# Attention with routed experts: one pair's transposes in each pair, VectorE's order written per pair

## The chip, the core and the metric

The kernel runs on one core of a Trainium2 chip. A core has engines with an instruction queue each: TensorE (PE; its weight loads are shown as PEld), VectorE (DVE), ScalarE (ACT), GpSimd (POOL) and SyncE (SP, which here only issues DMAs). They meet through semaphores. TensorE writes to PSUM, which has eight banks here handed out as named tiles. The metric is the device time of one execution in microseconds (us); lower is better.

## The reference

```python
scores = q @ k.T / sqrt(64); scores = cap * tanh(scores / cap)     # (8, 12, 448, 448)
attn = exp(scores - max) / (sum + 1e-9);  x = attn @ v             # x as (3584, 768)
logits = x @ w_gate + modality_bias[modality_id]                   # (3584, 8)
e_idx = argmax(logits); gate_w = softmax(logits)[e_idx]
for e in range(8):                                                 # 768 -> 1024 -> 768
    out[mask] = gate_w[mask, None] * (relu(x[mask] @ w1[e]) @ w2[e])
```

## The kernel before

**Attention** goes over 48 pairs of heads (g = 0 to 47; six pairs make a batch). Three pairs make a group h (HB = 3), two groups a batch; the odd group completes a batch, which is then routed. In pair g the four steps of the loop do this:

- Steps 0 and 2 issue the score matmuls of pair g (L453): queries and keys are split in a rounded part (hi) and the rest (lo), and three products are added. ScalarE takes each score block through tanh (L455, th) and exp (L457, pt, and sh for the keys that two heads share).
- Step 1 prepares pair g + 1 (prep: VectorE casts hi, L441, and subtracts lo, L442), adds up the exponentials of pair g - 1 (two additions to tot, L552 and L553), and multiplies them by the values (L462, weigh_own, into the PSUM tile xT).
- Step 3 adds the shared keys (L467, weigh_shared) and VectorE copies xT to SBUF (L572). The next pair's L462 needs that PSUM tile back. Then pair g + 2 is fetched.

A group of three pairs leaves over the next three pairs. In the first (r = 0) and second (r = 1), sums (L477) forms denominators and logits on TensorE (glog); at the end of the second, VectorE copies glog (L483), TensorE transposes it (L486, lt), and VectorE forms reciprocals and logits (L491, L494). For an odd group, route follows: a string of small VectorE operations (L210 to L234), and in the next pair a rank on TensorE (L238, L240), positions (L244 to L251), and four indirect writes to a map in DRAM by POOL (L264). In the third pair (r = 2), after L467, all three pairs are transposed (rows_out, L505, four transposes for each pair) and VectorE scales each result by the reciprocal into xs (L506); POOL then writes xs to DRAM (L515). The first and third set use the one PSUM buffer tp, the middle one the buffer "small", which rank and lt use too.

**The early slot.** After group 13 (pair 45), early_slot picks an expert that has a full block of rows. SP loads its first weights (raw; four buffers), POOL reads the map back (L653, mt) and gathers the rows (L660, xg). While the last pairs run, the weights are cast and split (split_w, L676 on ScalarE, L677 on VectorE; SPLITS says at which pair and step), and the gathered rows are transposed (L696; MOVES says where) into x (L703, L705, L706). Then the **experts** run (ffn1 L723 to L727, ffn2 L752), first with the early slot, then with the slots planned from the counts.

**What sets the order.** Python's order is the program's; the tile framework then orders each engine's instructions anew by its own estimates, except those marked with pin, which keep their order among each other. Before, all matmuls and DMAs issued by SP are pinned, and on VectorE only prep of the first two pairs and the early slot's casts. Tiles with n buffers (bufs) make the writer of the n + 1st wait for the readers of the first.

Of the kernel before, what the change touches and what calls it, by code (L numbers as in the profile page):

```python
# [39 lines left out]
F32 = mybir.dt.float32  # L40
# [4 lines left out]
ALU = mybir.AluOpType  # L45
# [4 lines left out]
B, H, S, D = 8, 12, 448, 64  # L50
C, CP = 4, 112
NP = H // 2
NT, DM, FF, E, NM = B * S, H * D, 1024, 8, 2
# [5 lines left out]
GW = 32  # L59
# [12 lines left out]
HB = 3  # L72
# [3 lines left out]
class Program:  # L76
# [7 lines left out]
    def pin(self, inst):  # L84
        return self.tc.keep_in_program_order(inst)
# [327 lines left out]
    def attention(self, qk, first, rp):  # L413
        tc, nc = self.tc, self.nc
        pe, pin = nc.tensor, self.pin
        with ExitStack() as st:
# [17 lines left out]
            def prep(g):  # L434
                kq, va = fetched.pop(g)
                hi = sp.tile([128, QK], F32R, name="hi")
                lo = sp.tile([128, QK], F32R, name="lo")
                keep = pin if g < 2 else (lambda inst: inst)

                for cs in (slice(0, QK),) if g else (slice(0, KC2), slice(KC2, QK)):  # L440
                    keep((nc.scalar.copy if cs.start else nc.vector.tensor_copy)(hi[:, cs], kq[:, cs]))  # L441
                    keep(nc.vector.tensor_tensor(lo[:, cs], kq[:, cs], hi[:, cs], op=ALU.subtract))  # L442
                return hi, lo, va
# [34 lines left out]

            def by_token():

                w = HB * GW
                gl = xp.tile([w, S], F32, name="gl")
                nc.vector.tensor_copy(gl, self.glog[:w, :S])  # L483
                lt = self.ps_r.tile([128, 512], F32, name="lt", tag="small")
                for c in range(C):
                    pin(pe.transpose(lt[:CP, c * w : (c + 1) * w], gl[:, c * CP : (c + 1) * CP], self.ident[:w, :w]))  # L486
                return lt[:CP, : C * w].rearrange("p (c t x) -> p c t x", c=C, t=HB)
# [11 lines left out]

            def rows_out(h, t, xs, rec):  # L500
                xT = kept.pop(h * HB + t)[0]
                pool, tag = (self.ps_r, "small") if t == 1 else (ps_v, "tp")
                tp = pool.tile([128, 512], F32, name="tp", tag=tag)
                for c in range(C):
                    pin(pe.transpose(tp[:CP, c * 128 : (c + 1) * 128], xT[:, c * CP : (c + 1) * CP], self.ident))  # L505
                nc.vector.tensor_tensor(  # L506
                    xs[:, :, t * 128 : (t + 1) * 128].rearrange("p c (j d) -> p c j d", j=2),
                    tp[:CP].rearrange("p (c j d) -> p c j d", c=C, j=2),
                    rec[:, :, t].unsqueeze(3).to_broadcast([CP, C, 2, D]),
                    op=ALU.mult,  # L510
                )

            def store(h, xs):
# [7 lines left out]
            SPLITS = {  # L521
                (NG - 2, 1): (0,),
                (NG - 2, 3): (1,),
                (NG - 1, 1): (2,),
                (NG - 1, 3): (3,),
                (NG - 0, 0): (4,),
                (NG - 0, 1): (5,),
            }
            MOVES = {(NG - 1, 3): (0, 1), (NG, 1): (2, 3), (NG, 3): (4, 5)}
            self.warm(self.ps_r, 4)  # L530
# [4 lines left out]
            fetch(1)  # L535
            kept, lgs, routing, raws = {}, {}, {}, []
            for g in range(NG + 1):
# [4 lines left out]
                for step in range(C):  # L542
# [3 lines left out]
                    if step == 1:  # L546
                        if g + 1 < NG:
                            ready = prep(g + 1)
                        if g:
                            ppt, psh, pva = pend  # L550
                            tot = xp.tile([128, 2, S], F32, name="tot", bufs=HB + 1)
                            nc.vector.tensor_tensor(tot, ppt[:, 0:2], ppt[:, 2:4], op=ALU.add)  # L552
                            nc.vector.tensor_tensor(tot, tot, ppt[:, 4:6], op=ALU.add)  # L553
                            xT = ps_x.tile([128, 512], F32, name="xT")
                            weigh_own(xT, ppt, pva)

                        if g > HB:
                            h, r = divmod(g - HB - 1, HB)
                            if r < 2:
                                sums(h, 2 * r)  # L560
                                sums(h, 2 * r + 1)
                    if step == 3:
                        if g in routing:
                            next(routing.pop(g), None)
                        if g == 3:
                            self.empty_map()
                        if g == 2:
                            self.gate_bias()
                        if g:
                            weigh_shared(xT, psh, pva)  # L570
                            xs_ = xp.tile([128, S], F32, name="xT", bufs=HB + 3)
                            nc.vector.tensor_copy(xs_, xT[:, :S])  # L572
                            kept[g - 1] = xs_, tot, psh
                        fetch(g + 2)
                        if g > HB:
                            h, r = divmod(g - HB - 1, HB)
                            b = h // NH
                            if r == 1:
                                if h % NH == 0:
                                    lgs[b] = xp.tile([CP, C, H, E], F32, name="lg")  # L580
                                lt = by_token()
                                rec = logits(h, lt, lgs[b])
                                if h % NH == NH - 1:
                                    way = self.route(b, lgs[b], rp, self.ps_r)
                                    next(way)
                                    routing[g + 1] = way
                            if r == 2:
                                xs = xp.tile([CP, C, HB * 128], F32, name="xs")
                                for t in range(HB):
                                    rows_out(h, t, xs, rec)  # L590
                                store(h, xs)
                                if h == NH * (B - 1) - 1:
                                    meta = self.early_slot(self.cpool, self.ps_r)
                    for k in SPLITS.get((g, step), ()):
# [7 lines left out]
                if g == NG - 3:  # L602
                    e = self.expert(meta, 0)
                    early = e, self.rows(meta, 0)
                    raws = [self.load_raw(e, self.w1, k, FF) for k in range(self.nstage)]
                if g == NG - 2:
                    self.gather(early[1], known=NT - S)
            self.raws = [self.load_raw(e, self.w2, k, DM) for k in range(self.nstage)]
            h = NG // HB - 1
            for part in range(4):  # L610
                sums(h, part)
            rec = logits(h, by_token(), lgs[B - 1])
            way = self.route(B - 1, lgs[B - 1], rp, self.ps_r)
# [322 lines left out]
    def build(self):  # L936
        tc, nc = self.tc, self.nc
        with ExitStack() as st:
# [4 lines left out]
            with ExitStack() as sa:  # L943
                qk = sa.enter_context(tc.tile_pool(name="qk", bufs=3))
                first = self.load_kq(qk, 0, parts=2)
# [90 lines left out]
```

## Time and profile before

| | us |
|---|---|
| runs | 1011.59, 1011.34, 1003.75 (median 1011.34) |
| the profiled execution | 1000.3 |
| its span, first to last instruction | 998.6 |
| PE busy in the span | 923.6 (92%) |
| DVE busy | 542.2 (54%) |
| ACT busy | 555.5 (56%) |
| POOL busy | 132.6 (13%) |
| mean granted clock of TensorE | 0.972 |

The span has two stages: attention up to about 469, the experts from there on. A row of a list gives line, engine, operation, what is written and read, count, busy time and mean duration, and after the bar the idle time of the engine ahead of these instructions and what ended it. A row of the timeline starts with start and duration; in brackets stands the idle time before it and its releaser. A busy TensorE is not TensorE at its peak, since the ends of matmuls are modelled.

### The profile page before, as it was taken

Reading aid. Unit: us, or ns where it says so; the run is one execution under the profiler, and the core shown is the slowest. Engines: PE = TensorE matmul, PEld = TensorE weight load, DVE = VectorE, ACT = ScalarE, POOL = GpSimd, SP = SyncE. Lnnn points to the kernel's source line nnn. Section 1 sums busy time; section 2 is a strip of 40 time slices with the busy share of each in tenths; the row PEclk is TensorE's granted clock in tenths of the full one; section 3 lists DMA queues with packets and bytes.
Section 4 is the critical chain, followed back from the end, with each engine's and each line's share of the span. In section 5 each row is a group of like instructions: output and inputs, shape, how many; then the busy total and the mean of one; then the engine's idle time right before and its main releaser. Section 6 shows DMA issues by size and latency. Waiting matters only on the chain. (4 is left out here: it accounts for less than half of the span.)

```text
span 998.6 us, 14505 instructions
## 1 busy us (share of the span) xinstructions
PE 923.6 (92%) x5360; PEld 709.6 (71%) x5360; DVE 542.2 (54%) x940; ACT 555.5 (56%) x759; POOL 132.6 (13%) x145
## 2 busy tenths in 40 slices
PE   8898989999898989876989999999999999999997
PEld 3444444444444444434879999999999999998987
DVE  5657676656556676646644444343434343428762
ACT  6877778867676777762334443443434443436551
POOL 1001002020202011031242020202020202011100
PEclk9999999999899999988999999999999999999998
DMA  3422424233233423264376363536353545347660
GB/s 114 133 90 92 140 99 118 96 113 119 89 119 85 123 91 121 97 155 138 92 254 226 123 209 118 206 132 199 131 193 131 182 145 182 131 137 248 230 199 6
DMA packets 47176, 139.98 MB, mean 140 GB/s; under 512 B 8686, under 2 KB 9198, under 8 KB 47088
## 3 DMA queue, kind: packets, MB, share of 16 engines
q1 hardware_dynamic: 38000, 105.78, 32.2%
q0 software_dynamic: 8944, 33.10, 11.0%
q8 instruction: 46, 0.75, 0.3%
q14 instruction: 42, 0.34, 0.1%
q10 hardware_dynamic: 144, 0.00, 0.0%
HBM read 117.35 MB, written 22.69 MB: 140 GB/s over the span
## 5 line engine op out<-in xcount | busy, mean ns | idle before, releaser
L455 ACT ACTIVATE th<-sc,isc 128x896 f32<-128x896 f32 x192 | 167.1, 907 | 105.8 <-PE sc L453 105.8
L727 PE MATMUL ph<-x,al 128*128 128x384 f32 (+2 forms) x528 | 167.9, 318 | 0.0
L752 PE MATMUL py<-bh,hh 128*128 128x384 f32 x464 | 159.6, 344 | 2.9 <-ACT hh L733 2.3
L752 PE MATMUL py<-bh,hl 128*128 128x384 f32 x464 | 156.0, 337 | 0.0
L752 PE MATMUL py<-bl,hh 128*128 128x384 f32 x464 | 155.7, 336 | 0.0
L457 ACT ACTIVATE pt<-th,cabs 128x896 f32<-128x896 f32 x144 | 148.0, 1043 | 1.9
L462 PE MATMUL xT<-pt,va 128*64 128x448 f32 x576 | 126.1, 575 | 6.5 <-DVE xT L572 6.5
L723 PE MATMUL ph<-x,ah 128*128 128x384 f32 x384 | 129.5, 337 | 0.5 <-DVE hl L734 0.5
L724 PE MATMUL ph<-x,ah 128*128 128x384 f32 x384 | 129.2, 336 | 0.0
L552 DVE TENSOR_TENSOR tot<-pt 128x896 f32<-128x896 f32 x48 | 52.4, 1091 | 122.3 <-ACT pt L457 68.9
L677 DVE TENSOR_TENSOR bl<-raw,bh 128x768 fp32r<-128x768 f32 x88 | 81.4, 955 | 56.2 <-ACT bh L676 55.4
L676 ACT CAST bh<-raw 128x768 fp32r<-128x768 f32 x88 | 70.2, 839 | 63.9 <-DMA raw<-in_w_dram 55.7
L727 PEld LDWEIGHTS ph<-x,al 128*128 128x128 f32 x528 | 102.1, 193 | 0.0
L453 PE MATMUL sc<-hi 64*128 64x448 f32 (+1 forms) x336 | 90.7, 469 | 6.7 <-ACT th L455 6.1
L677 DVE TENSOR_TENSOR al<-raw,ah 128x1024 fp32r<-128x1024 f32 x66 | 78.8, 1222 | 28.7 <-ACT ah L676 28.2
L453 PEld LDWEIGHTS sc<-hi 64*128 64x128 f32 (+1 forms) x336 | 38.4, 198 | 75.8 <-ACT pt L457 27.4
L462 PEld LDWEIGHTS xT<-pt,va 128*64 128x64 f32 x576 | 39.1, 144 | 74.6 <-issue 55.0
L752 PEld LDWEIGHTS py<-bh,hh 128*128 128x128 f32 x464 | 87.5, 189 | 4.0 <-ACT hh L733 2.9
L757 ACT ACTIVATE ot<-py,mt 128x384 f32<-128x384 f32 x58 | 33.6, 580 | 100.4 <-PE py L752 51.4
L752 PEld LDWEIGHTS py<-bl,hh 128*128 128x128 f32 x464 | 87.7, 189 | 0.0
L752 PEld LDWEIGHTS py<-bh,hl 128*128 128x128 f32 x464 | 87.5, 189 | 0.1
L676 ACT CAST ah<-raw 128x1024 fp32r<-128x1024 f32 x66 | 66.6, 1048 | 33.4 <-DMA raw<-in_w_dram 31.8
(159 smaller groups left out, 1302.8 us busy)
## 6 DMA issues: line engine op xcount, KB each, us to landing
raw<-in_w_dram SPq DMA_DIRECT2D x66, 512.0 KB, 5.1
raw<-in_w_dram SPq DMA_DIRECT2D x88, 384.0 KB, 4.8
kq<-in_kq_dram SPq DMA_DIRECT2D x47, 480.0 KB
va<-in_v_dram SPq DMA_DIRECT2D x48, 256.0 KB, 2.7
xd<-xs POOLq DMA_DIRECT2D x16, 672.0 KB
mapd<-pay,pos POOLq DMA_INDIRECT x32
xg<-xd,mt POOLq DMA_INDIRECT x30
out_dram<-ot,mt POOLq DMA_INDIRECT x29
```

The source lines that it names most:

```text
L453: pin(pe.matmul(sc[:, j, :S], k[rows, ks], q[rows, KC2:], start=i == 0, stop=i == 2))
L455: nc.scalar.activation(th[:, :n], sc[:, :n, :S], AF.Tanh, scale=self.isc)
L457: nc.scalar.activation(dst, th[:, :n] if step < KU else th[:, 0], AF.Exp, scale=self.cabs)
L462: pin(pe.matmul(xT[j * D : (j + 1) * D, :S], va[:, u * D : (u + 1) * D], pt[:, u], start=u < 2, stop=False))
L552: nc.vector.tensor_tensor(tot, ppt[:, 0:2], ppt[:, 2:4], op=ALU.add)
L676: a = self.nc.scalar.copy(hi, raw)
L677: b = self.nc.vector.tensor_tensor(lo, raw, hi, op=ALU.subtract)
L723: nc.tensor.matmul(ph[:, :w], hi[:, fs], self.x[:, k, 0, :w], start=first, stop=False)
L724: nc.tensor.matmul(ph[:, :w], hi[:, fs], self.x[:, k, 1, :w], start=False, stop=False)
L727: nc.tensor.matmul(ph[:, :w], lo[:, fs], self.x[:, k, 0, :w], start=False, stop=last)
L752: nc.tensor.matmul(py[:, :HALF], self.h[a][:, f, rows], self.w2s[f][c][:, cs], start=i == 0, stop=i == 3 * FC - 1,)
L757: nc.scalar.mul(ot[:, cs], py[:, :HALF], mt[:, t, 1:2])
```

## The change

- rows_out transposes one pair in each pair of the loop, where it did three in every third: set t of group h in pair 3h + 6 + t, ahead of the shared product, always through tp. The three at once stay for groups 13, 14 and 15 (`burst`). The store follows the third.
- VectorE's casts, additions, evictions and copies in the pair loop are all pinned, so their order is that of the text: hi, lo, two additions, (copy of glog), eviction, xT.
- tot has five buffers instead of four, the kept xT seven instead of six, qk (the loads of queries and keys) two instead of three.
- The early slot's casts come one step or pair later, its transposes all in the last turn of the loop, and the gather is written right after the loads.

```diff
-                keep = pin if g < 2 else (lambda inst: inst)
...
-                    keep((nc.scalar.copy if cs.start else nc.vector.tensor_copy)(hi[:, cs], kq[:, cs]))
-                    keep(nc.vector.tensor_tensor(lo[:, cs], kq[:, cs], hi[:, cs], op=ALU.subtract))
+                    pin((nc.scalar.copy if cs.start else nc.vector.tensor_copy)(hi[:, cs], kq[:, cs]))
+                    pin(nc.vector.tensor_tensor(lo[:, cs], kq[:, cs], hi[:, cs], op=ALU.subtract))
...
+            def copy_sums():
+                gl = xp.tile([HB * GW, S], F32, name="gl")
+                pin(nc.vector.tensor_copy(gl, self.glog[: HB * GW, :S]))
+                return gl
...
-            def rows_out(h, t, xs, rec):
+            def rows_out(h, t, xs, rec, burst=True):
                 xT = kept.pop(h * HB + t)[0]
-                pool, tag = (self.ps_r, "small") if t == 1 else (ps_v, "tp")
+                pool, tag = (self.ps_r, "small") if burst and t == 1 else (ps_v, "tp")
...
             SPLITS = {
-                (NG - 2, 1): (0,),
-                (NG - 2, 3): (1,),
-                (NG - 1, 1): (2,),
-                (NG - 1, 3): (3,),
-                (NG - 0, 0): (4,),
-                (NG - 0, 1): (5,),
+                (NG - 2, 3): (0,),
+                (NG - 1, 1): (1,),
+                (NG - 1, 3): (2,),
+                (NG, 0): (3,),
+                (NG, 1): (4,),
+                (NG, 2): (5,),
             }
-            MOVES = {(NG - 1, 3): (0, 1), (NG, 1): (2, 3), (NG, 3): (4, 5)}
+            MOVES = {(NG, 1): (0, 1), (NG, 2): (2, 3), (NG, 3): (4, 5)}
...
+            LAST = NH * (B - 1) - 1
...
-                            tot = xp.tile([128, 2, S], F32, name="tot", bufs=HB + 1)
-                            nc.vector.tensor_tensor(tot, ppt[:, 0:2], ppt[:, 2:4], op=ALU.add)
-                            nc.vector.tensor_tensor(tot, tot, ppt[:, 4:6], op=ALU.add)
+                            tot = xp.tile([128, 2, S], F32, name="tot", bufs=HB + 2)
+                            pin(nc.vector.tensor_tensor(tot, ppt[:, 0:2], ppt[:, 2:4], op=ALU.add))
+                            pin(nc.vector.tensor_tensor(tot, tot, ppt[:, 4:6], op=ALU.add))
...
+                        h, t = divmod(g - 2 * HB, HB)
+                        if h >= 0 and (t == 0 or h < LAST):
+                            if t == 0:
+                                rec, xs = recs.pop(h), xp.tile([CP, C, HB * 128], F32, name="xs")
+                            for u in (t,) if h < LAST else range(HB):
+                                rows_out(h, u, xs, rec, h >= LAST)
+                            if t == HB - 1 or h >= LAST:
+                                store(h, xs)
+                            if h == LAST:
+                                meta = self.early_slot(self.cpool, self.ps_r)
                         if g:
                             weigh_shared(xT, psh, pva)
-                            xs_ = xp.tile([128, S], F32, name="xT", bufs=HB + 3)
-                            nc.vector.tensor_copy(xs_, xT[:, :S])
+                            xs_ = xp.tile([128, S], F32, name="xT", bufs=2 * HB + 1)
+                            pin(nc.vector.tensor_copy(xs_, xT[:, :S]))
...
-                if g == NG - 2:
                     self.gather(early[1], known=NT - S)
...
-                qk = sa.enter_context(tc.tile_pool(name="qk", bufs=3))
+                qk = sa.enter_context(tc.tile_pool(name="qk", bufs=2))
```

TensorE in the third pair of an odd group, before: sc are scores, tp the transposes of the kept xT, rank the routing's.

```order
L453 MATMUL sc<-lo,hi 128x448
L238 LDWEIGHTS tri
L238 MATMUL rank<-oh,tri 112x32
L240 LDWEIGHTS ones
L240 MATMUL rank<-before,ones 112x32
L467 MATMUL xT<-sh,va 128x448
L505 MATMUL tp<-ident,xT 112x128 x12
L453 MATMUL sc<-hi 128x448 x2
```

The same place in the changed program:

```order
L452 MATMUL sc<-lo,hi 128x448
L238 LDWEIGHTS tri
L238 MATMUL rank<-oh,tri 112x32
L240 LDWEIGHTS ones
L240 MATMUL rank<-before,ones 112x32
L507 MATMUL tp<-ident,xT 112x128 x4
L466 MATMUL xT<-sh,va 128x448
L452 MATMUL sc<-hi 128x448 x2
```

Eight of the twelve transposes have left for the next two pairs, and the four that stay stand ahead of the shared product.

VectorE in that pair, before: acc ends the routing's string, rows and posf are its positions, xs the evictions.

```order
L552 TENSOR_TENSOR tot<-pt 128x896
L234 TENSOR_TENSOR acc<-before,oh 112x8
L259 TENSOR_REDUCE gs<-ex 112x4
L260 TENSOR_SCALAR gs<-gs 112x4
L441 CAST hi<-kq 128x960
L244 TENSOR_TENSOR rows<-rank,region 112x32
L261 RECIPROCAL pay<-gs 112x4
L442 TENSOR_TENSOR lo<-kq,hi 128x960
L247 TENSOR_TENSOR rows<-rows,oh 112x32
L572 COPY xT<-xT 128x448
L249 TENSOR_REDUCE posf<-rows 112x4
L506 TENSOR_TENSOR xs<-tp,rec 112x4x128
```

And in the changed program:

```order
L234 TENSOR_TENSOR acc<-before,oh 112x8
L440 CAST hi<-kq 128x960
L260 TENSOR_SCALAR gs<-gs 112x4
L441 TENSOR_TENSOR lo<-kq,hi 128x960
L555 TENSOR_TENSOR tot<-pt 128x896
L261 RECIPROCAL pay<-gs 112x4
L556 TENSOR_TENSOR tot<-tot,pt 128x896
L244 TENSOR_TENSOR rows<-rank,region 112x32
L508 TENSOR_TENSOR xs<-tp,rec 112x4x128
L247 TENSOR_TENSOR rows<-rows,oh 112x32
L588 COPY xT<-xT 128x448
```

Both additions now stand between lo and xT, and one eviction ahead of xT; the routing's string still stands ahead of hi.

ScalarE in pair 46, before: ah is the first cast of the early slot's weights.

```order
L457 ACTIVATE pt<-th,cabs 128x896
L676 CAST ah_149<-raw 128x1024
L455 ACTIVATE th<-sc,isc 128x896
L455 ACTIVATE th<-sc,isc 128x448
L457 ACTIVATE pt<-th,cabs 128x896
L457 ACTIVATE sh<-th,cabs 128x448
L676 CAST ah_151<-raw 128x1024
```

And in the changed program, from the end of pair 46 into pair 47:

```order
L456 ACTIVATE pt<-th,cabs 128x896
L456 ACTIVATE sh<-th,cabs 128x448
L682 CAST ah_149<-raw 128x1024
L454 ACTIVATE th<-sc,isc 128x896 x2
L456 ACTIVATE pt<-th,cabs 128x896 x2
L682 CAST ah_151<-raw 128x1024
```

The first cast has moved behind all of pair 46's activations.

More of the change, by code (lines that the diff above doesn't have):

```diff
@@ L477, in sums, with by_token @@
                     pin(pe.matmul(self.glog[t * GW : (t + 1) * GW, :S], w, rhs, start=part == 0, stop=part == 3))
-            def by_token():
+            def copy_sums():
+                gl = xp.tile([HB * GW, S], F32, name="gl")
+                pin(nc.vector.tensor_copy(gl, self.glog[: HB * GW, :S]))
+                return gl
+            def by_token(gl):
                 w = HB * GW
-                gl = xp.tile([w, S], F32, name="gl")
-                nc.vector.tensor_copy(gl, self.glog[:w, :S])
                 lt = self.ps_r.tile([128, 512], F32, name="lt", tag="small")
@@ L505, in rows_out @@
                     pin(pe.transpose(tp[:CP, c * 128 : (c + 1) * 128], xT[:, c * CP : (c + 1) * CP], self.ident))
-                nc.vector.tensor_tensor(
+                pin(nc.vector.tensor_tensor(
                     xs[:, :, t * 128 : (t + 1) * 128].rearrange("p c (j d) -> p c j d", j=2),
@@ L510, in rows_out @@
                     op=ALU.mult,
-                )
+                ))
             def store(h, xs):
@@ L535, in attention @@
             fetch(1)
-            kept, lgs, routing, raws = {}, {}, {}, []
+            kept, lgs, recs, routing, raws = {}, {}, {}, {}, []
+            LAST = NH * (B - 1) - 1
             for g in range(NG + 1):
@@ L561, in attention @@
                                 sums(h, 2 * r + 1)
+                                if r:
+                                    gl = copy_sums()
                     if step == 3:
@@ L569, in attention @@
                         if g:
                             weigh_shared(xT, psh, pva)
-                            xs_ = xp.tile([128, S], F32, name="xT", bufs=HB + 3)
-                            nc.vector.tensor_copy(xs_, xT[:, :S])
+                            xs_ = xp.tile([128, S], F32, name="xT", bufs=2 * HB + 1)
+                            pin(nc.vector.tensor_copy(xs_, xT[:, :S]))
                             kept[g - 1] = xs_, tot, psh
                         fetch(g + 2)
-                        if g > HB:
-                            h, r = divmod(g - HB - 1, HB)
+                        h, r = divmod(g - HB - 1, HB)
@@ L577, in attention @@
+                        if h >= 0 and r == 1:
                             b = h // NH
[L578 to L593, printed above, removed]
+                            if h % NH == 0:
+                                lgs[b] = xp.tile([CP, C, H, E], F32, name="lg")
@@ L594, in attention @@
+                            recs[h] = logits(h, by_token(gl), lgs[b])
+                            if h % NH == NH - 1:
+                                way = self.route(b, lgs[b], rp, self.ps_r)
+                                next(way)
+                                routing[g + 1] = way
                     for k in SPLITS.get((g, step), ()):
@@ L611, in attention @@
                 sums(h, part)
-            rec = logits(h, by_token(), lgs[B - 1])
+            rec = logits(h, by_token(copy_sums()), lgs[B - 1])
             way = self.route(B - 1, lgs[B - 1], rp, self.ps_r)
```

## The prediction

> **What bounds the kernel now.** I read the busy time by stage first: from the first transposes of sums (L486, at 54.64) to those of group 13 (413.60), and on to the first matmul of the experts (469.16). The columns are the stretch, its length, then busy time and instructions of PE, PEld, DVE, ACT and POOL, the granted clock, the DMA share and GB/s.
>
> ```profile
> 54.64:413.60 358.96, 324.29 (x1899) 164.65 (x1897) 228.15 (x401) 266.70 (x319) 39.76 (x43) 0.96 0.34 108
> 413.60:469.16 55.56, 39.59 (x221) 19.43 (x219) 33.93 (x71) 29.78 (x38) 12.34 (x11) 0.88 0.51 144
> ```
>
> TensorE (PE) is busy 90% of the attention stage, VectorE (DVE) 64%, ScalarE (ACT) 74%: TensorE sets the pace, and what stops it counts. The experts' 529 us behind 469.16 are not touched, so the change can win only in these two rows. Next, who stops TensorE between 54.64 and 413.60, from the list of waits:
>
> ```profile
> PE tp L505 <- DVE xs L506: 25.9, 13, 2.2
> PE xT L462 <- DVE xT L572: 4.0, 13, 0.3
> PE tp L505 <- DVE rows L244: 3.5, 6, 0.6
> PE rank L240 <- DVE before L233: 1.2, 6, 0.2
> ```
>
> That is 34.6 us, the whole of TensorE's idle time there (358.96 - 324.29 = 34.67). 29.4 of it stands before the three pairs' transposes (tp). The timeline shows why, in a pair in which an even group leaves:
>
> ```profile
> 219.99 0.47 PE L453 MATMUL sc<-hi 64*128 64x448 f32 x2
> ...
> 226.13 1.04 PE L505 MATMUL tp<-ident,xT 128*112 128x128 f32 x8
> 226.28 0.65 DVE L441 CAST hi<-kq 128x960 fp32r<-128x960 f32 x1
> 226.97 1.16 DVE L442 TENSOR_TENSOR lo<-kq,hi 128x960 fp32r<-128x960 f32 x1
> 228.04 0.62 DVE L572 COPY xT<-xT 128x448 f32<-128x448 f32 x1
> 228.57 1.28 DVE L506 TENSOR_TENSOR xs<-tp,rec 112x512 f32<-112x512 f32 x2
> 229.31 0.65 PE L505 MATMUL tp<-ident,xT 128*112 128x128 f32 x4 [2.15 <-DVE xs L506]
> 229.89 0.47 PE L453 MATMUL sc<-hi 64*128 64x448 f32 x2
> ...
> 231.31 0.97 PE L462 MATMUL xT<-pt,va 128*64 128x448 f32 x4
> ```
>
> The third set of transposes needs the first set's buffer, whose reader (xs, at 228.57) stands behind hi, lo and xT on VectorE. Then the groups one by one, from L486 to L486:
>
> ```profile
> 54.64:82.41 27.77, 25.31 (x147) 12.93 (x146) 16.06 (x23) 20.46 (x25) 0.90 (x1) 0.94 0.31 107
> 82.41:109.66 27.25, 24.32 (x149) 12.21 (x148) 19.30 (x42) 20.60 (x26) 6.03 (x6) 1.00 0.35 109
> ...
> 164.63:190.88 26.25, 23.81 (x147) 12.05 (x145) 16.06 (x23) 20.46 (x25) 0.72 (x1) 1.00 0.35 113
> 190.88:219.57 28.69, 25.79 (x149) 13.31 (x148) 19.30 (x42) 20.59 (x26) 5.64 (x6) 0.94 0.36 104
> ...
> 245.83:275.97 30.14, 27.24 (x148) 13.62 (x147) 19.27 (x42) 20.57 (x26) 5.30 (x6) 0.89 0.30 99
> ...
> 385.85:413.60 27.75, 25.29 (x147) 12.90 (x145) 16.05 (x23) 20.46 (x25) 0.72 (x1) 0.94 0.31 107
> ```
>
> There are 13 such rows, two kinds in turn: seven even ones, and six odd ones, whose batch is routed (42 VectorE instructions instead of 23). At a granted clock of 1.00 (six rows) an even one takes 26.25 and an odd one 27.25; at 0.94 (six rows) each is some 1.45 longer, at 0.89 (one row) 2.9. So eight slowdowns cost about 8 x 1.45 = 11.8 us (358.96 - 7 x 26.25 - 6 x 27.25 = 11.7).
>
> **The change part by part.**
>
> *Transposes in each pair.* No instruction is added or removed: 12 transposes and three evictions a group before and after. What goes is the wait for the buffer: 2.15 in an even group (the row at 229.31); in an odd one 25.9 - 7 x 2.15 = 10.9, or 1.8, and 3.5 / 6 = 0.6 for the rank that shares a buffer with the middle set. Since the buffer now has a whole pair to come free, I put the new wait at nothing. The cover is the pair itself: its shortest form is 219.99 to 226.13 on TensorE (6.1 us), and the eviction takes 0.64.
>
> *VectorE's order per pair.* It is now hi, lo, both additions, eviction, xT. The rows above give hi 0.65, lo 1.16, xT 0.62 and an eviction 0.64 (1.28 for two); the additions' groups:
>
> ```profile
> L552 DVE TENSOR_TENSOR tot<-pt 128x896 f32<-128x896 f32 x39 | 42.6, 1091 | 110.7 <-ACT pt L457 60.6 <-PE glog L477 50.1
> L553 DVE TENSOR_TENSOR tot<-tot,pt 128x896 f32<-128x896 f32 x39 | 41.5, 1063 | 0.0
> ```
>
> Together 5.2 us a pair, under the 6.1 of the shortest pair. xT, for which the next pair's L462 waits, was 0.3 late once a group; now the only work behind the shared product (L467) is xT itself, 0.62 against the 1.4 us of the next score matmuls (229.89 to 231.31 in the rows above). So that 4.0 goes too. The fifth tot buffer removes the 50.1 that VectorE waited for glog (L477), and that TensorE never felt: worth nothing alone, but without it the fixed order would hold xT behind an addition that waits for the group before.
>
> *The price of the order: routing.* In an odd group the routing's small operations now run ahead of hi in one queue. Their length, from the trace of before:
>
> ```profile
> 415.35 0.30 DVE L491 RECIPROCAL rec<-lt 112x24 f32<-112x24 f32 x1
> ...
> 421.02 0.66 DVE L441 CAST hi<-kq 128x960 fp32r<-128x960 f32 x1
> ```
>
> From rec to hi it is 5.67; two additions stood between, 2.15 by the groups, so 3.5 to 3.6 us are the routing's. In the pair after it VectorE has 3.6 + 5.2 + some 0.6 of rows, posf and pos = 9.4, and starts 0.4 after TensorE (rec waits for lt): xT is done at 9.8. TensorE's pair is 6.1 + 0.5 (one set of transposes, half of 1.04) + 0.4 (rank: 27.25 - 26.25 less its wait of 0.6) = 7.0, and wants xT 1.4 later, at 8.4. So a new wait of 1.4 in each odd group. Its bounds: nothing, if hi is not held; 2.4, if the routing takes the 5.67 less only one addition. I take 1.4, worked from the nearer rows.
>
> *The clock.* All seven slowed rows hold a burst of transposes with TensorE idle for 1.8 to 2.2 us; six bursts passed at 1.00. Afterwards transposes stand singly and the longest wait is 1.4. Bounds for the slowdowns left: none and all eight (11.8 us). I take one (1.5), because the new wait is shorter than every wait after which the clock fell.
> The Trainium skill ("TensorE: Matmul & The Clock Gate", Part 1 and Part 4) says the clock is halved after about one 3.4 us window without enough matmul work, and that transposes do not count as such work. By that rule no such window is left between 54.64 and 413.60 and the sum would be 1.5 lower; the same rule speaks against the end below, where TensorE idles longer than 3.4 us and would restart at half clock. The trace agrees so far as slowed rows follow bursts; that an idle window alone does it no row here isolates.
>
> Sum for this stage: 7 x (26.25 - 2.15 - 0.3) + 6 x (27.25 - 1.8 - 0.6 - 0.2 - 0.3 + 1.4) = 166.6 + 154.5 = 321.1, plus 1.5: 322.6 for 359.0, a gain of 36.4.
>
> *The end: casts later, gather.* Rows of the timelines, before:
>
> ```profile
> 436.16 1.04 ACT L676 CAST ah<-raw 128x1024 fp32r<-128x1024 f32 x1 [6.07 <-DMA raw<-in_w_dram]
> 438.17 0.74 PE L453 MATMUL sc<-hi 64*128 64x448 f32 x2 [5.20 <-ACT th L455]
> 440.03 0.61 POOL L653 DMA_DIRECT2D mt<-mapd  x1 [9.16 <-DMA mapd<-pay,pos]
> 446.69 3.41 POOL L660 DMA_INDIRECT xg<-xd,mt  x1 [5.89 <-issue]
> 457.24 0.75 PE L696 MATMUL ptr<-identr,xg 128*128 128x128 f32 x4 [2.06 <-DMA xg<-xd,mt]
> ```
>
> The first cast stopped ScalarE until its weights landed, and TensorE behind it for 5.20; one pair later it finds them there. But the 5.20 is not won: the early slot's rows still come through the same chain (map written, read back, gathered), and TensorE waits there. Without the 5.20 it would have begun pair 47 at 432.97; that pair, about 8.6 (half of 23.8 less the short pair's 6.6), and L462's 2.4 bring it to the gathered tiles near 444. The chain starts where it did (the pair of group 13 keeps its burst); POOL's order puts a 0.75 us store ahead of the map's writes, and two of the six first weight loads (they leave only when a cast frees a buffer) move out of its way. Bounds for the 457.24: no change, or the short waits that the trace has elsewhere (4.4, the longest of six in the pairs, for the 9.16; 3.59 at 507.90 for the 5.89; 1.05 there for the 3.41), together 9.4 earlier. I take the middle, 4.5 earlier.
>
> ```profile
> POOL pay L255 <- DMA mapd<-pay,pos: 14.0, 6, 4.4
> 507.90 1.05 POOL L660 DMA_INDIRECT xg<-xd,mt  x1 [3.59 <-DMA mt<-mapd]
> ```
>
> From the last gathered tile to the experts (469.16) it was 11.9; L462 leaves that stretch, but additions, two casts' differences and three evictions stand behind the tiles on VectorE, about 11 in sum: I put 0.7. Gain 5 in all, bounds 0 to 10.
>
> *The rest.* Two qk buffers for three: each load already leaves with the va load that waits for L467, so nothing; the cover is one pair.
>
> Total: 36.4 + 5 = 41.4 off the span of 998.6, or 957.2; with the 1.7 around it (the profiled execution took 1000.3) 959. That execution is 1.1% under the median, 1011.34; if the bursts that kept their clock in it lost it in those runs, 6 x 1.45 = 9 of the 11 us between them fall away with the bursts; if not, the median comes out near 970.
>
> **The rivals.**
> - *The clock still falls.* Routing's wait or the pair's edges slow it as often as before: 7 x 1.45 = 10, 969. For it: the clock fell in seven of 13 groups only, so bursts alone don't decide it. Against it: no slowed row is without its burst.
> - *The fixed order stops TensorE in every pair.* xT comes last on VectorE. If eviction and semaphores make it 0.5 later than L462 wants it, 39 x 0.5 = 20: 979. Against it: a margin of 0.8 (1.4 less 0.62).
> - *Nothing much moves* (within 1%): both of these, and no gain at the end, 959 + 10 + 20 + 5 = 994.
> - *Slower, by the single xs tile.* The next group's first eviction now comes one short pair (7 us) after the store of the last is issued, instead of three pairs; it stands in VectorE's queue ahead of xT. The traffic after a store:
>
> ```profile
> 233.00:236.00 3.00, 3.00 (x24) 0.89 (x20) 0.49 (x1) 1.88 (x2) 0.00 (x0) 1.00 0.73 229
> 236.00:237.60 1.60, 1.60 (x9) 0.86 (x5) 1.13 (x2) 1.33 (x2) 0.00 (x0) 1.00 0.00 0
> ```
>
> The store was issued at 231.75; its traffic is over by 236.0, 4.3 us later. A store of 12 us would cost 4.5 at each of 12 joins, 54: 1013. It decides from 7.5 us on.
>
> **How the numbers follow.** The forecast, 959 (its own bounds 945 to 971), has 0.62; the clock 0.13, the order 0.10, within 1% 0.07, slower 0.04; a larger gain, with no new wait and a gather 9 us sooner (below 942), 0.04. The range 942 to 982 holds the first three, 0.85, less some at their edges. Faster by over 1% (about what a measurement of this kernel can tell from no change): 0.89; within 1%: 0.07; slower: 0.04.
>
> **What would show it.** After: TensorE's waits for xs near nothing up to group 12; even groups near 23.8 us, odd ones near 25.8 with a wait L461 <- xT of 1 to 2; granted clock near 1.00 in that stage; the ScalarE wait for raw gone and TensorE's wait for xg grown to 8 or more. Wrong would be: waits for xT in every pair, VectorE waiting for a DMA at xs, or a clock of 0.95 as before.

## The result and the profile after

| | us |
|---|---|
| before, 4 runs beside the changed kernel | 1008.58 median (1003.75 to 1011.59) |
| after, 4 runs | 956.68 median (955.14 to 960.78) |
| ratio, 95% interval | 0.950 (0.944 to 0.955) |
| after, six more runs later | 958.10 median (954.87 to 960.67) |
| profiled execution, its span, mean granted clock | 955.14, 953.5, 0.979 |

The forecast was 959, with 942 to 982 around it. The stages of the changed kernel, first in the view of windows (columns as in the prediction): up to the first transposes of sums (L488 now), up to those of group 13, up to the first matmul of the experts, and the experts.

```profile
0.00:51.74 51.74, 46.11 (x231) 21.59 (x232) 30.37 (x50) 40.39 (x49) 4.88 (x19) 0.97 0.41 120
51.74:365.20 313.46, 306.39 (x1898) 155.21 (x1897) 234.42 (x400) 270.26 (x320) 39.12 (x42) 1.00 0.42 121
365.20:421.89 56.69, 39.40 (x221) 20.46 (x219) 36.59 (x73) 29.51 (x37) 11.88 (x12) 0.82 0.56 159
421.89:953.50 531.61, 511.46 (x3016) 502.21 (x3013) 248.01 (x418) 218.35 (x355) 75.74 (x72) 0.99 0.49 163
```

| stage | before | after | change | forecast |
|---|---|---|---|---|
| start | 54.64 | 51.74 | -2.9 | 0 |
| 13 groups of attention | 358.96 | 313.46 | -45.5 | -36.4 |
| end of attention | 55.56 | 56.69 | +1.1 | -5 |
| experts | 529.44 | 531.61 | +2.2 | 0 |
| span | 998.6 | 953.5 | -45.1 | -41.4 |

The sum came out near the forecast, but in part by luck: the stage of 13 groups beat its forecast by 9.1 and the start gave 2.9 that the sum didn't have, while the end missed by 6.1, the other way. The experts' code is the same in all kernels here and its stretch runs from 529 to 537 us between their profiles, so the 2.2 says nothing. Group by group, the attention stage now reads like this (two of 13 rows; the other even ones are 23.47 to 23.51, the other odd ones 24.81 to 24.86, all at a clock of 1.00):

```profile
75.23:100.08 24.85, 23.68 (x149) 12.06 (x147) 19.60 (x42) 20.83 (x26) 5.83 (x6) 1.00 0.41 120
...
341.69:365.20 23.51, 23.51 (x146) 11.93 (x145) 16.66 (x23) 20.70 (x25) 0.72 (x1) 1.00 0.38 126
```

In an even group TensorE is busy for the whole of its length. The list of waits of that stage has one row left for TensorE, in the six odd groups, where there were four rows with 34.6 us. VectorE now waits for the transposes instead of being waited for:

```profile
PE xT L461 <- DVE xT L588: 7.1, 6, 1.2
...
DVE xs L508 <- PE tp L507: 55.7, 32, 3.0
```

The end of attention, from the timeline. L702 transposes gathered tiles, L711 and L712 form x from them.

```profile
406.09 1.13 PE L702 MATMUL ptr<-identr,xg 128*128 128x128 f32 x7 [0.62 <-DMA xg<-xd,mt]
412.72 0.59 PE L702 MATMUL ptr<-identr,xg 128*128 128x128 f32 x3 [5.50 <-DVE x L712]
```

The last gathered tile is there at 406.09, 40.9 behind the transposes of sums (365.20); before, 43.6 (457.24 - 413.60). But then TensorE waits 5.50 for a low half of x. VectorE's own row of the timeline shows why:

```profile
399.34 1.08 DVE L555 TENSOR_TENSOR tot<-pt 128x896 f32<-128x896 f32 x1
407.76 0.56 DVE L712 TENSOR_TENSOR x<-ptr,x 128x384 fp32r<-128x384 f32 x1 [7.35 <-ACT x L711]
408.24 1.08 DVE L556 TENSOR_TENSOR tot<-tot,pt 128x896 f32<-128x896 f32 x1
409.24 1.22 DVE L683 TENSOR_TENSOR al<-raw,ah 128x1024 fp32r<-128x1024 f32 x1
410.37 0.55 DVE L709 CAST x<-ptr 128x384 fp32r<-128x384 f32 x1
```

The low half (L712) of the third column block, which waits for a cast on ScalarE, was put ahead of the second addition, of a weight's low half and of the casts of the first two blocks. Of the low halves in x, none is pinned; everything behind it is. So 7.35 us of VectorE passed idle, and what it could have done in them came after the gather.

### The profile page after: what moved, and what is told of

Its sections match the earlier page's. It is cut to its first block, busy times and chain, and to the rows that moved or that the text cites. A ratio compares the mean times of both kernels' runs of the same rounds, so it can differ in the third digit from the quotient of the medians.

```text
span 953.5 us, 14508 instructions
## 1 busy us (share of the span) xinstructions
PE 903.4 (95%) x5360; PEld 699.5 (73%) x5360; DVE 549.4 (58%) x940; ACT 558.5 (59%) x759; POOL 131.6 (14%) x145
## 5 line engine op out<-in xcount | busy, mean ns | idle before, releaser
L461 PE MATMUL xT<-pt,va 128*64 128x448 f32 x576 | 119.7, 551 | 8.7 <-DVE xT L588 7.1
L712 DVE TENSOR_TENSOR x<-ptr,x 128x384 fp32r<-128x384 f32 (+2 forms) x66 | 32.7, 517 | 100.1 <-ACT x L711 97.0
L452 PE MATMUL sc<-hi 64*128 64x448 f32 (+1 forms) x336 | 86.9, 446 | 2.7 <-ACT th L454 2.1
L461 PEld LDWEIGHTS xT<-pt,va 128*64 128x64 f32 x576 | 37.5, 137 | 69.2 <-issue 45.4
L739 ACT ACTIVATE hh<-ph 128x384 fp32r<-128x384 f32 x64 | 30.4, 489 | 94.4 <-PE ph L733 94.4
```

Of the source, the lines that this page charges most:

```text
L452: pin(pe.matmul(sc[:, j, :S], k[rows, ks], q[rows, KC2:], start=i == 0, stop=i == 2))
L461: pin(pe.matmul(xT[j * D : (j + 1) * D, :S], va[:, u * D : (u + 1) * D], pt[:, u], start=u < 2, stop=False))
L712: nc.vector.tensor_tensor(lo, pt[:, :w], hi, op=ALU.subtract)
```

## The experiments

Unless said otherwise each is the changed kernel with one edit. "Stage" is the stretch of 13 groups, "end" the one behind it. Times are medians of four or six runs beside the kernel before; the last two kernels have a single run.

**The transposes in a burst again, the order kept.**

```diff
-                            for u in (t,) if h < LAST else range(HB):
-                                rows_out(h, u, xs, rec, h >= LAST)
-                            if t == HB - 1 or h >= LAST:
+                            if t == 0:
+                                for u in range(HB):
+                                    rows_out(h, u, xs, rec)
+                            if t == 0:
                                 store(h, xs)
```

> The changed kernel with its transposes of three pairs in one burst again (in the first pair of a group), and with VectorE's fixed order, the buffers and the end as changed. The theory (the single transposes carry the gain; the fixed order alone leaves a wait for the buffer): even groups get back a wait for tp of 0.5 to 0.7, odd ones of about 2, since there the first eviction stands behind the late second addition; 7 x 0.6 + 6 x 2 = 16 us. If a burst is what slows the clock, it falls in about half of the groups again and adds 10: 983. If TensorE's idle time of about 2 us is what slows it, the even groups keep a granted clock of 1.00 and only odd ones fall: 973 to 978. The rival that the fixed order carries the gain: within 5 us of the changed kernel, 957 to 962.

Measured: 974.43 (972.51 to 977.90), inside the 973 to 978 of the second case. The stage takes 329.00, and the list of waits has

```profile
PE tp L507 <- DVE rows L244: 12.7, 6, 2.1
PE tp L507 <- DVE xs L508: 2.4, 7, 0.3
```

Even groups wait only 0.3 (2.15 in the kernel before, also in a burst), since hi, lo and xT no longer stand between the transposes and their eviction in VectorE's queue. Odd ones wait 2.1, because the middle transposes share a buffer with the rank, whose reader (rows, L244) stands behind both additions. From the windows, an even group, one of the three odd ones that lost the clock, and one of the three that did not:

```profile
153.37:177.41 24.04, 23.69 (x146) 11.97 (x145) 16.82 (x22) 20.45 (x25) 0.72 (x1) 1.00 0.40 123
177.41:204.94 27.53, 25.41 (x148) 12.85 (x147) 19.76 (x41) 20.57 (x26) 6.08 (x6) 0.94 0.39 109
...
331.94:358.05 26.11, 23.98 (x148) 12.05 (x147) 19.58 (x41) 20.59 (x26) 6.52 (x6) 1.00 0.47 114
```

The even group is at 1.00, burst and all, and so are the other six. So a burst with a wait of 0.3 does not slow the clock here.

**The order free again, the transposes single.** pin is taken off VectorE's hi, lo, both additions, the copies of glog and xT, and the eviction, as in this line:

```diff
-                            pin(nc.vector.tensor_copy(xs_, xT[:, :S]))
+                            nc.vector.tensor_copy(xs_, xT[:, :S])
```

> The changed kernel without the fixed order on VectorE (the scheduler puts hi, lo, additions, evictions and xT); transposes stay single, five buffers for additions. The theory (spread transposes carry the gain; the order is worth the 0.3 us by which xT was late once a group, and costs the 7.1 of routing): waits of TensorE for xT of 0.3 in 13 groups plus those of the first 50 us (2.5), no 1.2 in odd groups, so 957 with bounds 953 to 965; granted clock 1.00. The rival that the order carries much of the gain: above 970, with waits for xT in most pairs.

Measured: 977.33 (974.13 to 977.98); the expectation was wrong and the rival right. The stage takes 333.00 at a clock of 1.00. The waits for the transposes' buffer are gone here too, but TensorE waits for xT instead; the list of waits, and three rows of the timeline (L462 is the own share, L589 xT, numbers one higher than in the changed kernel):

```profile
PE xT L462 <- DVE xT L589: 22.1, 29, 1.9
...
DVE hi L441 <- PE sc L453: 34.7, 23, 2.7
```

```profile
328.19 0.66 DVE L441 CAST hi<-kq 128x960 fp32r<-128x960 f32 x1 [2.61 <-PE sc L453]
328.77 0.68 DVE L509 TENSOR_TENSOR xs<-tp,rec 112x512 f32<-112x512 f32 x1
329.37 1.15 DVE L442 TENSOR_TENSOR lo<-kq,hi 128x960 fp32r<-128x960 f32 x1
330.44 0.62 DVE L589 COPY xT<-xT 128x448 f32<-128x448 f32 x1
```

The free order puts hi early, where it waits for its buffer until the last score matmuls of the pair; eviction, lo and xT queue behind it, and xT ends 2.9 us after hi could start. In the fixed order xT stands ahead of the next hi. But this hi costs TensorE little: 0.34, as in the kernel before. TensorE's longest wait for xT, 1.89, stands behind a hi that waits for its load (kq):

```profile
331.11 2.48 PE L462 MATMUL xT<-pt,va 128*64 128x448 f32 x12 [0.34 <-DVE xT L589]
```

```profile
DVE hi L441 <- DMA kq<-in_kq_dram: 11.5, 8, 2.9
```

```profile
311.26 0.66 DVE L441 CAST hi<-kq 128x960 fp32r<-128x960 f32 x1 [2.88 <-DMA kq<-in_kq_dram]
...
314.17 2.48 PE L462 MATMUL xT<-pt,va 128*64 128x448 f32 x12 [1.89 <-DVE xT L589]
```

Eight such places make 9.7 of the 22.1. The kernel before has no wait of hi for a load; it also has three qk buffers where this one has two. The free order with three buffers was not run.

The two runs and the two kernels make a square (the stage, us; the kernel before also has its own buffers, and its transposes behind the shared product):

| | order free | order fixed |
|---|---|---|
| bursts | 358.96 (before) | 329.00 |
| single | 333.00 | 313.46 (after) |

Each half alone brings 26 to 30, the second 16 to 20 more. Two things are mixed into it. Of the 30.0 between the bursts some 7 are the clock: eight slowdowns (11.7) in the kernel before, three (1.4 each) with the order fixed. And of the 19.5 beside single transposes, up to 9.7 may belong to the third load buffer and not to the order.

**Four buffers for additions.**

```diff
-                            tot = xp.tile([128, 2, S], F32, name="tot", bufs=HB + 2)
+                            tot = xp.tile([128, 2, S], F32, name="tot", bufs=HB + 1)
```

> The changed kernel with four buffers for additions instead of five; the order of all instructions is the same. What the prediction claimed (the fixed order would hold xT behind an addition that waits for glog of the group before, 3.4 a group less 0.8 of slack in 13 groups): 990. The rival, from the place of the additions in the fixed order (an addition now comes a pair behind the sums that free its buffer): no wait, 957 as with five.

Measured: 960.04 (959.66 to 960.87), a stage of 314.02 against 313.46 and 314.64 in two profiles of the changed kernel. No wait of an addition for glog is listed in that stage. The prediction's claim about the fifth buffer falls, and the rival stands.

**The early slot's casts, moves and gather at their old places.** SPLITS, MOVES and the gather's place as on the minus side of the change.

> The changed kernel with the early slot's casts, moves and gather where they were in the kernel before. The prediction put these edits (the later casts, the earlier gather) at a gain of 5 us: then this runs in 962, and the stretch from group 13's transposes of sums to the experts takes 5 us more than the 56.7 of the changed kernel. The theory after its trace (the chain of the gather ends last either way; what the earlier gather won was lost in VectorE's queue): the stretch takes 55 to 58, with ScalarE waiting some 6 us for raw and TensorE 5 behind it, and the time is 955 to 959.

Measured: 962.97 (961.03 to 966.89), an end of 60.22. Beside the changed kernel's 56.69 the later casts and the earlier gather are thus worth 3.5 where the order is fixed (one profile each; by the times 3 against the kernel with four buffers, run beside it, and 5 to 6 against the changed kernel's own two sets). So the theory of this run was wrong, and the prediction's 5 is near as a number. Its reason is not borne out. With the gather at its old place the last tile is there 40.3 behind the transposes of sums (407.11 - 366.84), and POOL's waits for the map's writes and its read are 10.65 and 3.70, where they are 10.66 and 3.38 in the changed kernel:

```profile
407.11 0.75 PE L703 MATMUL ptr<-identr,xg 128*128 128x128 f32 x4 [1.02 <-DMA xg<-xd,mt]
```

With the free order and the new places (the run with the order free) it comes at 43.9:

```profile
433.02 1.13 PE L703 MATMUL ptr<-identr,xg 128*128 128x128 f32 x7 [0.54 <-DMA xg<-xd,mt]
```

The end thus has a square of its own (us, one profile each):

| order, places of the early slot | transposes of sums to the last tile | last tile to the experts | end |
|---|---|---|---|
| free, old (before) | 43.64 | 11.92 | 55.56 |
| fixed, old (this run) | 40.27 | 19.95 | 60.22 |
| free, new | 43.86 | 13.08 | 56.94 |
| fixed, new (after) | 40.89 | 15.80 | 56.69 |

The new places did not bring the last tile earlier under either order. What they save lies behind it, 4.2 in the fixed order and nothing in the free one. The fixed order makes that last stretch longer, by 8.0 at the old places and 2.7 at the new ones; the kernels with the old places differ in their buffers too. The last tile came 3.0 to 3.4 earlier with it, and the reason for that is not shown; in the runs below it comes as late as 44.1 with the order fixed. TensorE's waits for VectorE behind the last tile are 5.0 in this run (1.72, 1.64 and 1.63) and 0.48 in the kernel before. One place in VectorE's queue: the second addition of the last pair runs behind the gathered tiles' low halves (row 1, this kernel), while the free order had it done ahead of the gather (row 2, the kernel before, where the last tile came at 457.24).

```profile
416.58 1.08 DVE L556 TENSOR_TENSOR tot<-tot,pt 128x896 f32<-128x896 f32 x1
```

```profile
449.82 1.02 DVE L553 TENSOR_TENSOR tot<-tot,pt 128x896 f32<-128x896 f32 x1
```

**The changed kernel again, and two mends.**

> The changed kernel once more, beside the next three on the same chip: 957, a span of 953.5.

Measured: 958.10 (954.87 to 960.67). The first mend:

```diff
+                            late = g in routing
+                            if not late:
-                            pin(nc.vector.tensor_tensor(tot, tot, ppt[:, 4:6], op=ALU.add))
+                                pin(nc.vector.tensor_tensor(tot, tot, ppt[:, 4:6], op=ALU.add))
...
                             pin(nc.vector.tensor_copy(xs_, xT[:, :S]))
+                            if late:
+                                pin(nc.vector.tensor_tensor(tot, tot, ppt[:, 4:6], op=ALU.add))
```

> The changed kernel with the second addition behind the xT copy in the pairs that follow a routing. The theory (in odd groups xT is late because routing's operations and both additions stand ahead of it in VectorE's queue): TensorE's wait for xT falls from 1.2 to 0.1 or 0.2 in six groups, odd groups from 24.85 to 23.8, the time by 6: 951. The rival (the lateness only moves on to the next pair's xT, or ScalarE waits for the buffer that the second addition frees): no change, 957.

Measured: 953.16 (952.72 to 953.64). Odd groups take 24.21, the wait for xT is 3.2 in six (0.5 each): 0.65 of the 1.08 moved is won in each; the first addition and the routing's rows still stand ahead of xT. The cause of the wait is confirmed, the gain was overrated: the stage is 309.70, 3.8 to 4.9 less than in the changed kernel's two profiles. The end of this profile is 58.38. The second mend:

```diff
-        nc.vector.tensor_tensor(lo, pt[:, :w], hi, op=ALU.subtract)
+        low = nc.vector.tensor_tensor(lo, pt[:, :w], hi, op=ALU.subtract)
+        if pool is not getattr(self, "ps_t", None):
+            self.pin(low)
```

> The changed kernel with the early slot's low halves of x (the subtraction behind each cast) kept in program order on VectorE, so that none of a later tile stands ahead of the casts of the first two tiles. The theory (TensorE's wait of 5.5 us for x at 412.7 comes from that order: a low half that waits for ScalarE's cast held the second addition, a weight's low half and both casts behind it): the wait falls to 1.5 or so, the end by 3 to 4: 953. The rival (the gathered tiles or the weights' low halves set the end anyway): within 1 us, 957.

Measured: 955.64 (951.02 to 960.62), not to be told from 958.10. Its profile shows the wait mended and the gathered tiles later:

```profile
409.24 1.13 PE L702 MATMUL ptr<-identr,xg 128*128 128x128 f32 x7 [1.05 <-DMA xg<-xd,mt]
412.00 0.60 PE L702 MATMUL ptr<-identr,xg 128*128 128x128 f32 x3 [1.63 <-DVE x L712]
```

The wait for x fell from 5.50 to 1.63 as expected, and the stretch from the last tile to the experts from 15.8 to 12.3. But the last tile came 44.1 behind the transposes of sums (365.13) instead of 40.9, and the end is 56.41.

Then both mends in one kernel:

> Both edits together, the late second addition and the kept order of the low halves. They touch different stages, so the gains add: 6 + 4 = 10, or 947. The rivals: either of the two is worth nothing, 951 or 953.

Measured: 951.37 (948.21 to 953.88), stage 309.70, end 55.00, the last tile at 43.25. Less was gained than the expected 947; beside the first mend's 953.16 the second adds nothing that is clear of the spread.

**Why the gather came late in the last two.** The low half of the fifth weight now ran 7 us earlier, gave a weight buffer back, and a further weight load could run beside the gather. To test this theory, that cast and low half go behind the first two moves:

```diff
+                    early_moves = MOVES.get((g, step), ()) if step == 1 else ()
+                    for k in early_moves:
+                        self.transpose(k, (ps_s, self.ps_r)[k % 2], ("sc", "small")[k % 2], busy=k < 2)
                     for k in SPLITS.get((g, step), ()):
...
-                    for k in MOVES.get((g, step), ()):
+                    for k in () if early_moves else MOVES.get((g, step), ()):
```

> Both edits as before (late second addition, kept order of the low halves of x), and the fifth weight's cast and low half behind the casts of the first two gathered tiles. The theory (in the kernel with both edits that low half is freed from VectorE's queue 7 us earlier, gives back a weight buffer, and the next weight load then runs beside the gather, which lands 1.4 to 3 us later after group 13's transposes of sums): the last gathered tile lands 41 to 42 behind those transposes instead of 42.3 to 44.1, the wait for x stays at 1.6, and the stretch to the experts falls from 55.0 to 53 or 54: 949 to 951. The rival (the gather's landing varies by itself from run to run by as much): no change, 951.4, with a landing of 42 or more.

Measured: 953.30 (948.80 to 957.09); the last tile came 42.9 behind (404.61 - 361.71), the end is 56.73. The theory falls; the rival stands. Over the twelve profiles with the gather at its new place the landing lies between 40.4 and 44.1 (42.4 with the first mend alone), and what moves it stays open.

**Both additions behind xT after a routing**, on top of that:

```diff
+                            late = g in routing
+                            if not late:
+                                pin(nc.vector.tensor_tensor(tot, ppt[:, 0:2], ppt[:, 2:4], op=ALU.add))
+                                pin(nc.vector.tensor_tensor(tot, tot, ppt[:, 4:6], op=ALU.add))
...
                             pin(nc.vector.tensor_copy(xs_, xT[:, :S]))
+                            if late:
+                                pin(nc.vector.tensor_tensor(tot, ppt[:, 0:2], ppt[:, 2:4], op=ALU.add))
+                                pin(nc.vector.tensor_tensor(tot, tot, ppt[:, 4:6], op=ALU.add))
```

> The kernel before this one, with both additions behind the xT copy in the pairs that follow a routing. The theory (VectorE's queue ahead of xT is all that makes it late): the wait for xT that is left there, 0.5 in each of six groups, goes, odd groups fall from 24.21 to 23.7 and the time by 3 against the kernel before this one. The rival (the additions then give ScalarE its buffer back too late, and TensorE waits for scores or pt): odd groups stay or get longer, up to 1 us each, 0 to 6 us slower.

Measured: 948.45 (947.42 to 950.53), a ratio of 0.946 (0.943 to 0.950) to the kernel before. It is the lowest time of all, though not clear of the two mends together (0.947, 0.942 to 0.952, on another chip). Windows: the stage, the end.

```profile
52.92:359.70 306.78, 306.25 (x1898) 155.02 (x1897) 235.38 (x400) 269.46 (x320) 42.94 (x42) 1.00 0.45 124
359.70:414.57 54.87, 38.91 (x221) 19.79 (x219) 36.62 (x73) 29.41 (x37) 11.83 (x12) 0.84 0.67 165
```

TensorE idles 0.5 us in 306.78, once, for the copy of glog; the wait for xT is gone. The stage is 2.9 less than the 309.68 of the run before this one, near the six times 0.5.

**What slows the clock.** Two kernels take apart the burst and the idle time. In the first VectorE copies xT several times in one pair of each group (the value is the same); transposes are single.

```diff
+                        again = (3 if g in routing else 6) if HB < g < NG - 3 and g % HB == 0 else 1
...
-                            pin(nc.vector.tensor_copy(xs_, xT[:, :S]))
+                            for _ in range(again):
+                                pin(nc.vector.tensor_copy(xs_, xT[:, :S]))
```

> The changed kernel with VectorE copying xT six times in one pair of each even group and three times in the pair behind a routing, instead of once (the value is the same), so that TensorE idles once a group for 2.3 to 2.4 us without any burst of transposes: 7 x 2.3 + 6 x 1.2 = 23 us more, 980, if the clock holds. If TensorE's idle time of about 2 us is what slowed the clock in the kernel before, it falls again in about half of the groups, a granted clock of 0.94 to 0.96 in the stage, and 10 us more: 990. If it took the burst of transposes, it stays at 1.00 in every group.

Measured, one run: 1004.02. The waits, a group that lost the clock and the one that didn't, with the matmuls behind the wait in each (L461; L590 is xT):

```profile
PE xT L461 <- DVE xT L590: 33.3, 13, 2.6
```

```profile
162.74:191.81 29.07, 26.49 (x146) 12.50 (x145) 19.79 (x28) 20.67 (x25) 0.72 (x1) 0.88 0.33 102
...
302.73:328.94 26.21, 23.68 (x148) 11.99 (x147) 20.91 (x44) 20.81 (x26) 5.80 (x6) 1.00 0.65 97
```

```profile
173.87 4.75 PE L461 MATMUL xT<-pt,va 128*64 128x448 f32 x12 [2.58 <-DVE xT L590]
...
313.91 2.48 PE L461 MATMUL xT<-pt,va 128*64 128x448 f32 x12 [2.53 <-DVE xT L590]
```

Twelve of 13 groups fell, to 0.94 or 0.88, where half had been expected: the same twelve matmuls take 4.75 instead of 2.48. No burst is needed.

In the second the first pair's transposes are done three times over, so that twelve stand in a row without a wait:

```diff
-                    pin(pe.transpose(tp[:CP, c * 128 : (c + 1) * 128], xT[:, c * CP : (c + 1) * CP], self.ident))
+                    for _ in range(3 if t == 0 and not burst else 1):
+                        pin(pe.transpose(tp[:CP, c * 128 : (c + 1) * 128], xT[:, c * CP : (c + 1) * CP], self.ident))
```

> The changed kernel with the first pair's transposes of each group done three times into the same tile, so that twelve stand in a row as in the kernel before, but without the wait for a buffer between them. Eight more transposes at 0.13 are 1.04 a group; in odd groups the wait for xT hides them: 8 us more, 965, if the clock holds. If a burst alone slows the clock, it falls in about half of the groups, and 10 us more: 975. If it takes idle time, 1.00 in every group.

Measured, one run: 964.19; twelve transposes take 1.50, and every one of the 13 groups is at 1.00, with 0.9 as the longest idle time. So it is the idle time that slows the clock here, not the burst.

## Why the prediction was right, and where it was not

- **The waits for the transposes' buffer go** (29.4 of 34.6): right; none is left up to group 12. What the prediction missed is that the single transposes don't do it alone. It laid 29.4 to them and only 4.0 to the fixed order. The square shows the order worth 10 to 19.5 beside single transposes (the load buffers are mixed in) and 30.0 beside bursts, some 7 of it the clock. The wait for tp that it read at 229.31 was itself made by the queue (hi, lo and xT ahead of the eviction, in the very rows it quoted), and without the fixed order xT takes tp's place as what is late.
- **No wait in the shortest pair, for 5.2 us of VectorE's work under 6.1**: right; even groups leave TensorE no idle time.
- **The price of routing, 1.4 in each odd group**: 1.2 measured, at the place named. Moving one addition took away 0.65, moving both all of it.
- **The rest of the 9 us by which the stage beat its forecast** (45.5 against 36.4): the slowdown that was kept (1.5) did not come; even groups came to 23.5 where 23.8 was forecast, odd ones to 24.85 where 25.75 was. In an odd group 0.2 of it is the wait; 0.64 is TensorE's busy time (24.32 in the row 82.41, 23.68 in the row 75.23), whose fall the prediction had put at nothing; its cause was not followed.
- **The clock**: the reason given, waits too short to slow it, held, and the two kernels above show it. The rule of the Trainium skill ("TensorE: Matmul & The Clock Gate", Part 1), half speed after one window of about 3.4 us, gave no slowdown at all for this stage, which is what came. As a bound for a single idle time it does not hold here: 2.5 to 2.6 us did it in 12 of 13 groups, 2.1 in three of six.
- **The fifth buffer, "without it the fixed order would hold xT"**: wrong. In the fixed order an addition comes a pair behind the sums that free its buffer; the 50.1 us that VectorE waited before, in the free order, do not come back with four buffers.
- **The start, called unchanged**: 2.9 shorter. The row below, from the first 54.64 us of the kernel before, was overlooked: xT was late there as in the groups. With the order free and all else changed the wait is there again (2.6, a start of 56.16); with the order fixed 0.4 or less is left, and the start takes 51.7 to 53.3 in the other profiles.

```profile
PE xT L462 <- DVE xT L572: 2.5, 4, 1.6
```

- **The end, 5 less**: wrong, 1.1 more, and this is the step that failed. Its sum had 4.5 for an earlier gather and 0.7 for the stretch from the last tile to the experts. The last tile came 2.7 earlier, but not for the reason given: in the fixed order it came as early with the gather at its old place, and in the free order the new place brought nothing. The stretch behind it did not lose 0.7 but grew by 3.9, from 11.9 to 15.8. The fixed order was priced in the pairs only, and nothing had been asked of VectorE's queue behind the gather, where an unpinned low half got in front and TensorE waited 5.50. With the low halves kept in order 3.5 of the 3.9 went. ScalarE's wait for raw did go, as forecast (6.07 to 0.67). The sign given for this step, a wait of TensorE for xg grown to 8 or more, told nothing: it is 7.8, and was 7.6 before.
- **From one execution to the median**: the prediction had two values, 959 if the slowdowns that the profiled execution was spared fall away in the others, and 970 if not. The first came: the median, 956.68, is 1.5 above the profiled execution, where it was 8 to 11 above before. No trace of the other executions shows their groups. Over the eleven runs of the kernel before beside the last two mends, the longest (1019.33) has the lowest mean granted clock, 0.955, and the shortest (995.71) the highest, 0.975.
- **The single xs tile**: in the first profile no wait for a store; in the second one of 1.1 at one of 12 joins, and one of 1.7 with four buffers for additions. The rival was sound in kind and far from its 7.5 us. The two qk buffers cost nothing in the fixed order, as put.

## What to carry to other kernels

When a wait is put down to one instruction, look at what stands ahead of its releaser in that engine's queue: here the same wait could be shortened by asking later or by queueing better, and either alone left part of it, at this tile or at the next. An order fixed by hand must be priced at every stage that it runs through, the ends above all, since an instruction left free among pinned ones can hold all of them. When a stage is the sum of an arrival and what runs behind it, measure both: here the two moved against each other. A short wait of TensorE costs twice once it is long enough to slow the clock.

## What was not expected of the hardware

The longest single idle time of TensorE in a group against the groups that lost the clock: none at 1.2 (six in the changed kernel) and at 1.9 (one, with the free order); 1.8 to 2.2, seven of 13 in the kernel before; 2.1, three of six (all with a burst); 2.5 to 2.6, 12 of 13 without one. A loss costs some 1.4 us (26.11 against 27.53). At about 2 us of idle time equal groups of one execution thus fell on either side; what decides it is not shown.
